# A decode step's tail: the MLP weights in two transfers, and its first layer moved among the steps that join the softmax parts

## The chip, the cores and the metric

The kernel runs on one NeuronCore of one Trainium2 chip. Its engines have their own instruction streams and meet at semaphores: TensorE (PE in the profile) multiplies matrices into the accumulator memory PSUM, VectorE (DVE) reduces and works elementwise, ScalarE (ACT) applies functions, GpSimd (POOL) does little here, SyncE (SP) issues the transfers. Sixteen DMA engines move data from the chip's memory into the on-chip memory SBUF. The metric is the device time of one execution in microseconds, lower is better.

## The reference

One decode step of two branches that share the input `x` (2 x 1 x 448), mixed by a gate that depends on `x`:

```python
q = (x @ wq) per head                       # wq: 448 x (16 x 256)
scores = q . k_cache * 256 ** -0.5          # k_cache: 2 x 16 x 4096 x 256
p = softmax(scores)
a = concat_heads(p @ v_cache) @ wo          # v_cache like k_cache; wo: 4096 x 448
b = relu(x @ w1) @ w2                       # w1: 448 x 1792, w2: 1792 x 448
g = sigmoid(sum(x * gate_w))
out = g * a + (1 - g) * b
```

All is float32. The two caches are by far the most data: 32 pairs of batch row and head, each with 4 MB of keys and 4 MB of values.

## The kernel before

**Units.** A pair of batch row and head is a unit; there are U = 32, run one after another. A unit's keys and values come in one transfer of 8192 KB into one of three slots (`slot[0..2]`, each 128 partitions x 65,536 bytes). PE computes the scores (L121): the 4096 positions lie as four groups of 1024, each with 32 equal rows, so `sc` is 128 x 1024. DVE takes the maximum (L135, into `nm`), ACT the exponential and its row sum (L128, into `p` and `ls`), and DVE multiplies `p` into eight pieces of the values with a running sum (L141, into `ov`). So each unit leaves partial maxima, sums and outputs for four groups of positions in `nm`, `ls` and `ov`, which are joined once at the end. The semaphore `freed` counts the units that are done; SP waits for it before it issues the transfer that reuses a slot (L166 in the loop, L169 to L172 for the last two units; the last unit comes as keys and values apart).

**The weights that follow.** When unit U-2 (counted from one) has freed slot 0, SP issues the MLP's matrices into it, both in one transfer `wm` (L174, semaphore `mlp_in`). When unit U-1 has freed slot 1, it issues the output matrix `wo` in six transfers (L178): 32 chunks of 448 columns, as 14 and 9 (`ACC`) and 4, 2, 2, 1 (`DIRECT`), each with a semaphore of its own (`wo_in`). All of these stand in one queue behind the cache's transfers. The last instruction of SP waits for the result and writes it out (L181).

**The tail, in PE's written order.** The order of each engine's work is the order in which the program lists it.

1. L225 to L234: wait for `wm`, then the first layer, 16 matmuls (32 instructions, as each float32 matmul is recorded as two) into `pa`; `c` runs over four pieces of the 448 inputs, `g` over four groups of hidden columns.
2. ACT: `hs` = relu, scaled by 1 - g (L315). PE: transposes of `hs` into `pb` (L237, L239). ACT: copies to `hr` (L317, L320).
3. L242 to L244: wait for the last unit (`freed` = U), then transposes of `nm` and `ls` into `pc`.
4. The joining: DVE takes the overall maximum per unit (`nb`, L352), ACT the factors `e` (L325, written behind the copies to `hr`), DVE the sum, its reciprocal and the weights `wb` (L354 to L358), PE spreads `wb` over the partitions by a matmul into `pa` (L255), DVE multiplies it into `ov` (`os`, L360), PE sums the four groups (L261), DVE expands the result to the operand `oc` (L363).
5. The second layer (L250), 14 matmuls into `acc`, is written in three portions: before L255, before L261 and after it.
6. The output matrix's first 23 chunks add to the same `acc` (L275), which holds four partial results in four groups of rows. DVE copies it to `a_sb` (L367). The matmul with `fold` (L283) adds the groups up into `z`.
7. The last 9 chunks go to `z` directly (L288), 8 instructions for each. `FOLD_AT = 1` puts L283 behind the first four of these chunks and ahead of the other five. DVE copies `z` to `res` (L369).

Of the kernel before, what the change touches and what calls it, by code (L numbers as in the profile page):

```python
# [4 lines left out]
AF = mybir.ActivationFunctionType  # L5
# [5 lines left out]
G = 4  # L11
# [2 lines left out]
CW = 512  # L14
ACC = (14, 9)
DIRECT = (4, 2, 2, 1)
FOLD_AT = 1


def gated_mix_decode(nc, wq, kv, wm, wo, out):  # L20
# [23 lines left out]
    def ev():  # L44
        sems.append(nc.alloc_semaphore(f"e{len(sems)}"))
        return sems[-1]
# [13 lines left out]

    out_sem = nc.alloc_semaphore("out_sem")
    slot_in = [ev() for _ in range(SLOTS)]
    last_v, mlp_in = ev(), ev()
    wo_in = [ev() for _ in ACC + DIRECT]
    scored, maxed, raised, queried, freed = (ev() for _ in range(5))

# [88 lines left out]
    with nc.Block(no_gpsimd_drain=True) as block:  # L155

        @block.sync
        def _(_e):
            sp.wait_ge(q_mm, 2)
            sp.dma_start(slot[0], kv[2]).then_inc(slot_in[0], 16)  # L160
            with nc.Fori(0, LOOP - 1, engines=(ET.SP,)) as r:
                u0 = sp.snap(r * SLOTS)
                for k in range(SLOTS):
                    s = (k + 1) % SLOTS
                    sp.wait_ge(freed, u0 + k + 1)
                    sp.dma_start(slot[s], kv[bass.ds(u0 + k + SLOTS, 1)].rearrange("o p n -> (o p) n")  # L166
                                 ).then_inc(slot_in[s], 16)
            sp.wait_ge(freed, U - 4)
            sp.dma_start(slot[1], kv[U - 2]).then_inc(slot_in[1], 16)  # L169
            sp.wait_ge(freed, U - 3)  # L170
            sp.dma_start(slot[2][:, :SW // 2], kv[U - 1][:, :SW // 2]).then_inc(slot_in[2], 16)
            sp.dma_start(slot[2][:, SW // 2:], kv[U - 1][:, SW // 2:]).then_inc(last_v, 16)  # L172
            sp.wait_ge(freed, U - 2)
            sp.dma_start(slot[0][:, :wm.shape[1]], wm).then_inc(mlp_in, 16)  # L174
            sp.wait_ge(freed, U - 1)
            k = 0
            for n, s in zip(ACC + DIRECT, wo_in):
                sp.dma_start(w_o[:, k * D:(k + n) * D], wo[:, k * D:(k + n) * D]).then_inc(s, 16)  # L178
                k += n
            sp.wait_ge(res_ok, 1)  # L180
            sp.dma_start(out, res[0:7 * 15 + 1:7, :]).then_inc(out_sem, 16)  # L181
# [8 lines left out]
        @block.tensor  # L190
        def _(_e):
            pe.wait_ge(x_ok, 1)
            for c in range(KC):
                r = rows_of(c)
                m = pe.matmul(pa[:, :1], x_of(r, c, P), xg[r, c, B:], start=(c == 0), stop=(c == KC - 1))  # L195
            m.then_inc(gate_mm, 1)
            W = 2 * KF * DH
            for i in range(2):
                w = slot[0][:, i * NW // 2:(i + 1) * NW // 2]
                if i:  # L200
                    pe.wait_ge(q_ok, i)
# [12 lines left out]
                for k in range(2 * T):  # L214
                    m = pe.transpose(pc[:, k * P:(k + 1) * P], q[:, k * P:(k + 1) * P], ident)
                m.then_inc(q_tr, 1)
            with nc.Fori(0, LOOP, 1, engines=(ET.PE,)) as r:
                for k in range(SLOTS):
                    s = (k + 1) % SLOTS
                    unit_pe(k, r * SLOTS + (k + 1), r * 16 + (32 if s == 0 else 16), s)  # L220
            for k in range(U - U1):
                s = (k + 1) % SLOTS
                unit_pe(k, U1 + k + 1, LOOP * 16 + 16, s)

            pe.wait_ge(mlp_in, 16)  # L225
            half = W1 // 2
            for c in range(KC):
                for g in range(G):
                    j, i = divmod(g, 2)
                    at = i * half + (j * KF + c if c < KF else 2 * KF) * FG  # L230
                    r = rows_of(c, j)
                    m = pe.matmul(pa[g * R:(g + 1) * R, :FG], x_of(r, c), w1[r, at:at + FG], start=(c == 0),  # L232
                                  stop=(c == KC - 1))
            m.then_inc(hid_mm, 1)  # L234
            pe.wait_ge(hid_ok, 1)
            for t in range(KF):
                pe.transpose(pb[:, t * P:(t + 1) * P], hs[:, t * P:(t + 1) * P], ident)  # L237
            for j in range(2):
                m = pe.matmul(pb[j * HP:(j + 1) * HP, KF * P:], hs[:, KF * P:], ident, start=True, stop=True)  # L239
            m.then_inc(hid_tr, 1)  # L240

            pe.wait_ge(freed, U)  # L242
            pe.transpose(pc[:U, :P], nm, ident)
            pe.transpose(pc[:U, P:2 * P], ls, ident).then_inc(ml_tr, 1)  # L244
            pe.wait_ge(hr_ok, 1)

            def mlp(lo, hi):
                for k in range(lo, hi):
                    g = k % G
                    pe.matmul(acc[g * R:(g + 1) * R, :D], hr[:, k, :], w2[:, k * D:(k + 1) * D], start=(k < G),  # L250
                              stop=False)

            mlp(0, 4)
            pe.wait_ge(wb_ok, 1)
            pe.matmul(pa[:, :U], wb.rearrange("u g r -> u (g r)"), ident[:U, :U], start=True,  # L255
                      stop=True).then_inc(wp_mm, 1)
            mlp(4, 8)
            pe.wait_ge(os_ok, 1)
            n = HH * B * J
            for g in range(G):  # L260
                m = pe.matmul(pc[g * R:(g + 1) * R, :n], sel,  # L261
                              os.rearrange("p u j -> p (u j)")[:, g * n:(g + 1) * n], start=True, stop=True)
            m.then_inc(po_mm, 1)
            mlp(8, NF)

            def o_of(k):
                return oc[:, k // J, k % J].rearrange("p r b -> p (r b)")

            pe.wait_ge(oc_ok, 1)
            k, n = 0, sum(ACC)  # L270
            for i, a in enumerate(ACC):
                pe.wait_ge(wo_in[i], 16)
                for _ in range(a):
                    g = k % G
                    m = pe.matmul(acc[g * R:(g + 1) * R, :D], o_of(k), w_o[:, k * D:(k + 1) * D], start=False,  # L275
                                  stop=(k >= n - G))
                    k += 1
            m.then_inc(acc_mm, 1)
            for i, a in enumerate(DIRECT):
                if i == FOLD_AT:  # L280
                    pe.wait_ge(a_ok, 1)
                    for g in range(G):
                        pe.matmul(z[g * R:(g + 1) * R, :DG], fold.rearrange("p r b -> p (r b)"), a_sb[:, g * DG:(g + 1) * DG], start=False,  # L283
                                  stop=False)
                pe.wait_ge(wo_in[len(ACC) + i], 16)
                for _ in range(a):
                    for g in range(G):
                        m = pe.matmul(z[g * R:(g + 1) * R, :DG], o_of(k),  # L288
                                      w_o[:, k * D + g * DG:k * D + (g + 1) * DG], start=(k == n),
                                      stop=(k == NO - 1))  # L290
                    k += 1
            m.then_inc(z_mm, 1)

        @block.scalar
        def _(_e):
# [15 lines left out]
                    unit_act(u, u + 1, (k + 1) % SLOTS, (k + 2) % SLOTS)  # L311
            for u in range(U1, U):
                unit_act(u, u + 1, (u + 1) % SLOTS, (u + 2) % SLOTS, u == U - 1)
            act.wait_ge(hid_mm, 1)
            act.activation(hs, pa[:, :FG], AF.Relu, scale=omg).then_inc(hid_ok, 1)  # L315
            act.wait_ge(hid_tr, 1)
# [8 lines left out]
            act.activation(e, pc[:U, 0:P:R], AF.Exp, bias=nb, scale=-1.0).then_inc(e_ok, 1)  # L325

        @block.vector
        def _(_e):
# [28 lines left out]
            dve.wait_ge(rl_ok, 1)  # L357
            dve.tensor_scalar(wb, e[:, :, None].to_broadcast([U, G, R]), rl, gp[:U], op0=ALU.mult, op1=ALU.mult).then_inc(wb_ok, 1)  # L358
            dve.wait_ge(wp_mm, 1)
            dve.tensor_tensor(os, ov, pa[:, :U, None].to_broadcast([P, U, J]), op=ALU.mult).then_inc(os_ok, 1)  # L360
            dve.wait_ge(po_mm, 1)
            for h in range(HH):
                m = dve.tensor_copy(oc[:, h], pc[:, h * B * J:(h + 1) * B * J].rearrange("p (o b j) -> p j o b", o=1, b=B)  # L363
# [66 lines left out]
```

## Time and profile before

| what | value |
|---|---|
| median of 3 runs | 677.75 us (677.21 to 677.79) |
| the profiled execution | 677.45 us |
| its span, first to last instruction | 675.9 us |
| moved by the main queue | 289.55 MB, 99.1% of 16 engines' span |
| busy: PE, DVE, ACT | 211.9, 340.4, 46.4 us |
| mean granted TensorE clock | 0.669 |

A busy engine is not the same as a late one: what counts is the chain of waits that ended last. In the rows of a timeline the first number is the start in us from the span's start, the second the duration, then engine, line, operation, tile written and tiles read, shapes and count. In the chain of waits the rows are start, duration, what. A DMA issue row gives the count, KB of each, and the us from issue to landing. A window's row gives its length, the busy time and instruction count of PE, of PE's weight loads (PEld), DVE, ACT and POOL, then the granted TensorE clock as a share of full speed, the DMA engines' share and GB/s.

### The profile page before, as it was taken

The page shows a single profiled execution, that of the slowest core. Times are in us where ns is not written, and L with a number is a line of the kernel's source. Part 1 is how long each engine was busy: PE and PEld are TensorE (multiplying, and loading weights), DVE is VectorE, ACT ScalarE, POOL GpSimd, SP SyncE. Part 2 cuts the span into 40 slices and gives each one's busy share as a digit, 9 for nine tenths or more (in the row PEclk, how much of TensorE's full clock was granted, in tenths as well). Part 3 has the DMA queues.
Part 4 walks back from the last instruction along what each step waited for, and adds up shares of the span by engine and source line. Part 5 has one row for each costly group of instructions (what it writes and reads, how often), then busy time and mean ns, then how long its engine had stood idle before and what let it go on. Part 6 is the DMA issues. An engine that isn't in the chain of part 4 may idle for free.

```text
span 675.9 us, 3969 instructions
## 1 busy us (share of the span) xinstructions
PE 211.9 (31%) x1309; PEld 52.0 (8%) x1309; DVE 340.4 (50%) x563; ACT 46.4 (7%) x107; POOL 0.7 (0%) x6
## 2 busy tenths in 40 slices
PE   0742211323332122333322133333212333332427
PEld 0210000000000000000000000000000000000003
DVE  0015566554455666445556654545566554465742
ACT  0010000000000000000000000000000000000101
POOL 0000000000000000000000000000000000000000
PEclk9976567677665667766566776765567676665659
DMA  9999999999999999999999999999999999999996
GB/s 380 434 431 435 431 434 434 434 434 434 434 434 434 434 434 434 434 434 434 434 434 434 434 434 434 434 434 434 434 434 434 434 434 434 434 434 431 449 407 275
DMA packets 5940, 289.61 MB, mean 429 GB/s; under 512 B 688, under 2 KB 816, under 8 KB 1200
## 3 DMA queue, kind: packets, MB, share of 16 engines
q1 hardware_dynamic: 5936, 289.55, 99.1%
q8 instruction: 3, 0.05, 0.0%
q14 instruction: 1, 0.01, 0.0%
HBM read 289.54 MB, written 0.01 MB: 428 GB/s over the span
## 4 chain that ended last, share of the span: by engine, by line
DMA 69%; PE 12%; DVE 12%; issue 6%; DVEq 1%; ACT 1%; ACTq 0%; SPq 0%
DMA slot<-in_kv 61%; DVE slot L141 9%; PE sc L121 8%; DMA slot<-in_wm 5%; DMA slot<-in_wq 3%; DVE nm L135 2%; PE pb L206 1%; PE pa L232 1%; PE acc L275 1%; DVEq L141 1%; ACT p L128 0%; PE pa L195 0%; PE z L288 0%; DVE oc L363 0%; ACTq L307 0%
## 5 line engine op out<-in xcount | busy, mean ns | idle before, releaser
L141 DVE SCALAR_TENSOR_TENSOR slot<-slot,p 128x1024 f32<-128x1024 f32 x256 | 295.9, 1221 | 47.1 <-ACT p L128 47.1
L121 PE MATMUL sc<-slot,qc 128*32 128x512 f32 x1024 | 181.5, 874 | 419.4 <-DMA slot<-in_kv 419.4
L135 DVE TENSOR_REDUCE nm<-sc 128x1024 f32 (+1 forms) x32 | 39.2, 1225 | 243.9 <-PE sc L121 243.9
L121 PEld LDWEIGHTS sc<-slot,qc 128*32 128x32 f32 x1024 | 41.0, 153 | 559.2 <-issue 539.7
L128 ACT ACTIVATE p<-sc,nm 128x1024 f32<-128x1024 f32 x32 | 35.7, 1114 | 563.2 <-DVE nm L135 563.2
L141 DVE DVE_READ_ACCUMULATOR slot<-slot,p (+1 forms) x256 | 21.2, 83 | 0.0
L232 PE MATMUL pa<-slot,xr 128*32 128x448 f32 (+1 forms) x32 | 5.4, 826 | 18.7 <-DMA slot<-in_wm 18.7
L206 PE MATMUL pb<-slot,xr 128*32 128x512 f32 (+1 forms) x64 | 10.0, 763 | 0.0
L335 DVE COPY xr<-slot 128x512 f32<-128x512 f32 x1 | 0.4, 427 | 18.1 <-DMA slot<-in_wq 18.1
L195 PE MATMUL pa<-slot,xr 128*128 128x1 f32 (+1 forms) x8 | 1.9, 356 | 20.8 <-DVE xr L335 20.8
L352 DVE TENSOR_REDUCE nb<-pc 32x1 f32<-32x4 f32 x1 | 0.1, 149 | 12.6 <-PE pc L244 12.6
L128 ACT ACTIVATION_READ_ACCUMULATOR p<-sc,nm (+1 forms) x32 | 6.2, 193 | 0.0
L130 ACT ACTIVATE qc<-qt 128x2 f32 (+1 forms) x31 | 6.0, 192 | 0.0
L275 PE MATMUL acc<-slot,oc 128*32 128x448 f32 x46 | 4.7, 541 | 0.0
L250 PE MATMUL acc<-slot,hr 128*32 128x448 f32 x28 | 3.5, 546 | 0.6 <-ACT hr L320 0.6
L195 PEld LDWEIGHTS pa<-slot,xr 128*128 128x128 f32 (+1 forms) x8 | 1.8, 320 | 20.8 <-DVE xr L335 20.8
L367 DVE COPY a_sb<-acc 128x448 f32<-128x448 f32 x1 | 0.6, 625 | 4.8 <-PE acc L275 4.8
L232 PEld LDWEIGHTS pa<-slot,xr 128*32 128x32 f32 (+1 forms) x32 | 1.1, 150 | 23.1 <-DMA slot<-in_wm 19.6
L206 PEld LDWEIGHTS pb<-slot,xr 128*32 128x32 f32 (+1 forms) x64 | 2.0, 129 | 6.4 <-issue 6.3
L288 PE MATMUL z<-slot,oc 128*32 128x112 f32 x72 | 2.5, 260 | 0.0
L315 ACT ACTIVATE hs<-pa,omg 128x448 f32<-128x448 f32 x1 | 0.6, 634 | 19.9 <-PE pa L232 19.9
L288 PEld LDWEIGHTS z<-slot,oc 128*32 128x32 f32 x72 | 2.0, 110 | 0.5 <-issue 0.5
(45 smaller groups left out, 17.8 us busy)
## 6 DMA issues: line engine op xcount, KB each, us to landing
slot<-in_kv SPq DMA_DIRECT2D x2, 4096.0 KB, 34.5
slot<-in_wq SPq DMA_DIRECT2D x1, 7174.0 KB, 19.6
slot<-in_wm SPq DMA_DIRECT2D x1, 6272.0 KB, 36.3
slot<-in_wo SPq DMA_DIRECT2D x1, 3136.0 KB, 24.2
slot<-in_wo SPq DMA_DIRECT2D x1, 2016.0 KB, 28.6
slot<-in_wo SPq DMA_DIRECT2D x1, 896.0 KB, 30.2
slot<-in_wo SPq DMA_DIRECT2D x2, 448.0 KB, 31.2
slot<-in_kv SPq DMA_DIRECT2D x31, 39.9
```

The source lines that it names most:

```text
L121: m = pe.matmul(sc[g * R:(g + 1) * R, c * CW:(c + 1) * CW], qc[:, s, t:t + 1].to_broadcast([P, R]), slot[s][:, lo:lo + CW], start=(t == 0) ...
L128: act.activation(p, sc, AF.Exp, bias=nm[:, bass.ds(u, 1)], accum_out=ls[:, bass.ds(u, 1)]).then_inc(raised, 1)
L130: act.activation(qc[:, s_next, :], qt[:, bass.ds(u + 1, 1), :].rearrange("p o t -> p (o t)"), AF.Copy).then_inc(queried, 1)
L135: dve.tensor_reduce(nm[:, bass.ds(u, 1)], sc, axis=AX.X, op=ALU.max, negate=True).then_inc(maxed, 1)
L141: m = dve.scalar_tensor_tensor(v, v, 1.0, p, op0=ALU.mult, op1=ALU.mult, accum_out=ov[:, bass.ds(u, 1), j].rearrange("p o -> p o"))
L195: m = pe.matmul(pa[:, :1], x_of(r, c, P), xg[r, c, B:], start=(c == 0), stop=(c == KC - 1))
L206: m = pe.matmul(pb[g * R:(g + 1) * R, :], x_of(r, c), w[r, at:at + CW], start=(c == 0), stop=(c == KC - 1))
L232: m = pe.matmul(pa[g * R:(g + 1) * R, :FG], x_of(r, c), w1[r, at:at + FG], start=(c == 0), stop=(c == KC - 1))
L250: pe.matmul(acc[g * R:(g + 1) * R, :D], hr[:, k, :], w2[:, k * D:(k + 1) * D], start=(k < G), stop=False)
L275: m = pe.matmul(acc[g * R:(g + 1) * R, :D], o_of(k), w_o[:, k * D:(k + 1) * D], start=False, stop=(k >= n - G))
L288: m = pe.matmul(z[g * R:(g + 1) * R, :DG], o_of(k), w_o[:, k * D + g * DG:k * D + (g + 1) * DG], start=(k == n), stop=(k == NO - 1))
L315: act.activation(hs, pa[:, :FG], AF.Relu, scale=omg).then_inc(hid_ok, 1)
```

## The change

The MLP's matrices come in two transfers with a semaphore each, `w1` first. The first layer is written ahead of the joining: its first two pieces of inputs stand before the wait for the last unit, the third between the transposes of `nm` and `ls` and the wait for `wb`, the fourth between the `wb` matmul and the wait for `os`. The sum over groups (L261 before) follows, then relu, transposes and copies, and the second layer in one piece behind the waits for `w2` and `hr`. The `wb` matmul goes to `pb` instead of `pa`, since `pa` is in use by the first layer; DVE reads it there. ACT's `e` stands ahead of the relu. `FOLD_AT` is 0: the folded sums come ahead of all direct chunks, and start the sum in `z`. The number of matmuls is the same.

```diff
-FOLD_AT = 1
+FOLD_AT = 0
...
-            sp.dma_start(slot[0][:, :wm.shape[1]], wm).then_inc(mlp_in, 16)
+            sp.dma_start(w1, wm[:, :W1]).then_inc(w1_in, 16)
+            sp.dma_start(w2, wm[:, W1:]).then_inc(w2_in, 16)
...
-            pe.wait_ge(mlp_in, 16)
             half = W1 // 2
...
-            m.then_inc(hid_mm, 1)
+
+            def hidden(lo, hi):
+                for c in range(lo, hi):
+                    for g in range(G):
+                        j, i = divmod(g, 2)
+                        at = i * half + (j * KF + c if c < KF else 2 * KF) * FG
+                        r = rows_of(c, j)
+                        m = pe.matmul(pa[g * R:(g + 1) * R, :FG], x_of(r, c), w1[r, at:at + FG], start=(c == 0),
+                                      stop=(c == KC - 1))
+                return m
+
+            pe.wait_ge(w1_in, 16)
+            hidden(0, 2)
+            pe.wait_ge(freed, U)
+            pe.transpose(pc[:U, :P], nm, ident)
+            pe.transpose(pc[:U, P:2 * P], ls, ident).then_inc(ml_tr, 1)
+            hidden(2, 3)
+            pe.wait_ge(wb_ok, 1)
+            pe.matmul(pb[:, :U], wb.rearrange("u g r -> u (g r)"), ident[:U, :U], start=True,
+                      stop=True).then_inc(wp_mm, 1)
+            hidden(3, 4).then_inc(hid_mm, 1)
+            pe.wait_ge(os_ok, 1)
+            n = HH * B * J
+            for g in range(G):
+                m = pe.matmul(pc[g * R:(g + 1) * R, :n], sel,
+                              os.rearrange("p u j -> p (u j)")[:, g * n:(g + 1) * n], start=True, stop=True)
+            m.then_inc(po_mm, 1)
             pe.wait_ge(hid_ok, 1)
             for t in range(KF):
                 pe.transpose(pb[:, t * P:(t + 1) * P], hs[:, t * P:(t + 1) * P], ident)
...
-            pe.wait_ge(freed, U)
-            pe.transpose(pc[:U, :P], nm, ident)
-            pe.transpose(pc[:U, P:2 * P], ls, ident).then_inc(ml_tr, 1)
+            pe.wait_ge(w2_in, 16)
             pe.wait_ge(hr_ok, 1)
...
-            mlp(0, 4)
-            pe.wait_ge(wb_ok, 1)
...
-            mlp(4, 8)
-            pe.wait_ge(os_ok, 1)
...
-            mlp(8, NF)
+            for k in range(NF):
+                g = k % G
+                pe.matmul(acc[g * R:(g + 1) * R, :D], hr[:, k, :], w2[:, k * D:(k + 1) * D], start=(k < G),
+                          stop=False)
...
-                                      w_o[:, k * D + g * DG:k * D + (g + 1) * DG], start=(k == n),
+                                      w_o[:, k * D + g * DG:k * D + (g + 1) * DG], start=(k == n and FOLD_AT > 0),
...
+            act.wait_ge(nb_ok, 1)
+            act.activation(e, pc[:U, 0:P:R], AF.Exp, bias=nb, scale=-1.0).then_inc(e_ok, 1)
             act.wait_ge(hid_mm, 1)
             act.activation(hs, pa[:, :FG], AF.Relu, scale=omg).then_inc(hid_ok, 1)
...
-            act.wait_ge(nb_ok, 1)
-            act.activation(e, pc[:U, 0:P:R], AF.Exp, bias=nb, scale=-1.0).then_inc(e_ok, 1)
...
-            dve.tensor_tensor(os, ov, pa[:, :U, None].to_broadcast([P, U, J]), op=ALU.mult).then_inc(os_ok, 1)
+            dve.tensor_tensor(os, ov, pb[:, :U, None].to_broadcast([P, U, J]), op=ALU.mult).then_inc(os_ok, 1)
```

More of the change, by code (lines that the diff above doesn't have):

```diff
@@ L62, in gated_mix_decode @@
     slot_in = [ev() for _ in range(SLOTS)]
-    last_v, mlp_in = ev(), ev()
+    last_v, w1_in, w2_in = ev(), ev(), ev()
     wo_in = [ev() for _ in ACC + DIRECT]
@@ L223, in _ @@
                 unit_pe(k, U1 + k + 1, LOOP * 16 + 16, s)
-            pe.wait_ge(mlp_in, 16)
             half = W1 // 2
[L227 to L233, printed above, removed]
-            m.then_inc(hid_mm, 1)
+            def hidden(lo, hi):
[23 more added lines that the diff above has]
+            m.then_inc(po_mm, 1)
             pe.wait_ge(hid_ok, 1)
@@ L240, in _ @@
             m.then_inc(hid_tr, 1)
-            pe.wait_ge(freed, U)
-            pe.transpose(pc[:U, :P], nm, ident)
-            pe.transpose(pc[:U, P:2 * P], ls, ident).then_inc(ml_tr, 1)
+            pe.wait_ge(w2_in, 16)
             pe.wait_ge(hr_ok, 1)
[L247 to L251, printed above, removed]
-            mlp(0, 4)
-            pe.wait_ge(wb_ok, 1)
-            pe.matmul(pa[:, :U], wb.rearrange("u g r -> u (g r)"), ident[:U, :U], start=True,
-                      stop=True).then_inc(wp_mm, 1)
-            mlp(4, 8)
-            pe.wait_ge(os_ok, 1)
[L259 to L263, printed above, removed]
-            mlp(8, NF)
+            for k in range(NF):
+                g = k % G
+                pe.matmul(acc[g * R:(g + 1) * R, :D], hr[:, k, :], w2[:, k * D:(k + 1) * D], start=(k < G),
+                          stop=False)
             def o_of(k):
@@ L282, in _ @@
                     for g in range(G):
-                        pe.matmul(z[g * R:(g + 1) * R, :DG], fold.rearrange("p r b -> p (r b)"), a_sb[:, g * DG:(g + 1) * DG], start=False,
-                                  stop=False)
+                        pe.matmul(z[g * R:(g + 1) * R, :DG], fold.rearrange("p r b -> p (r b)"),
+                                  a_sb[:, g * DG:(g + 1) * DG], start=(i == 0), stop=False)
                 pe.wait_ge(wo_in[len(ACC) + i], 16)
```

## The prediction

> **What bounds the kernel now.** I read the page first, then the chain of waits in order of time from the last cache units on, then the timeline of the same stretch, the DMA issues with their landings, and last the windows for the granted clock.
>
> ```profile
> span 675.9 us, 3969 instructions
> ...
> q1 hardware_dynamic: 5936, 289.55, 99.1%
> ```
>
> One queue keeps its engines busy for 99.1% of the span. 289.55 MB are unchanged by the edit, so only what stands behind the last bytes, or between them and the end, can be won. The chain of the last 60 us:
>
> ```profile
> 618.61 36.30 DMA slot<-in_wm
> ...
> 654.96 5.42 PE pa L232 x32
> ...
> 660.40 0.64 ACT hs L315
> ...
> 661.09 0.55 PE pb L237 x3
> ...
> 662.05 0.49 ACT hr L317
> ...
> 662.90 0.26 ACT e L325
> ...
> 663.56 0.34 DVE wb L358
> 663.95 0.40 PE pa L255 x2
> ...
> 665.42 1.43 DVE oc L363 x4
> ...
> 666.89 4.08 PE acc L275 x41
> ```
>
> The whole MLP transfer lands at 618.61 + 36.30 = 654.91. From there it is one serial chain on PE, ACT and DVE (first layer, relu, transposes, softmax joining, expansion into `oc`), until L275 may start at 666.89. The tail of it, from the timeline:
>
> ```profile
> 671.66 0.62 DVE L367 COPY a_sb<-acc 128x448 f32<-128x448 f32 x1 [4.82 <-PE acc L275]
> 672.34 0.40 PE L283 MATMUL z<-a_sb,fold 128*32 128x112 f32 x8
> 672.56 1.14 PE L288 MATMUL z<-slot,oc 128*32 128x112 f32 x40
> 673.77 0.28 DVE L369 COPY res<-z 128x112 f32<-128x112 f32 x1 [1.48 <-PE z L288]
> 674.07 0.60 SPq L181 DMA_DIRECT2D out<-res  x1
> ```
>
> The last z matmul ends at 672.56 + 1.14 = 673.70; 2.2 us later the span is over, and 1.55 us lie outside it (the profiled execution took 677.45). Against it stand the landings of the output matrix. The issues one after another, from the timeline of SP, and then the DMA issues with their sizes and the us to landing (a median where there are two):
>
> ```profile
> 638.15 0.33 SPq L178 DMA_DIRECT2D slot<-in_wo  x1
> 638.52 0.43 SPq L178 DMA_DIRECT2D slot<-in_wo  x1
> 639.00 0.43 SPq L178 DMA_DIRECT2D slot<-in_wo  x1
> 639.47 0.43 SPq L178 DMA_DIRECT2D slot<-in_wo  x1
> 639.94 0.91 SPq L178 DMA_DIRECT2D slot<-in_wo  x2
> ```
>
> ```profile
> slot<-in_wo SPq DMA_DIRECT2D x1, 3136.0 KB, 24.2
> slot<-in_wo SPq DMA_DIRECT2D x1, 2016.0 KB, 28.6
> slot<-in_wo SPq DMA_DIRECT2D x1, 896.0 KB, 30.2
> slot<-in_wo SPq DMA_DIRECT2D x2, 448.0 KB, 31.2
> ...
> slot<-in_wo SPq DMA_DIRECT2D x1, 224.0 KB, 31.5
> ```
>
> Issue plus landing gives: A0 (14 chunks) 662.35, A1 (9) 667.12, D0 (4) 669.20, D1 and D2 (2 each) about 670.67 and 671.14, D3 (1) 640.42 + 31.5 = 671.92, where 640.42 is 639.94 + 0.91 - 0.43. So A0 lies there for 4.5 us before L275 begins, and at D3's landing PE still has the fold and 40 z matmuls ahead. The end is now set by the chain, by 673.70 - 671.92 = 1.78 us over the last landing. That is the most that the edit can touch.
>
> **The change part by part.** *The split transfer.* One more issue on SP, 0.33 us by the row of the first L178 issue. It stands behind the wait for unit U-2 (618.61) and ahead of the wait that ends at 638.15, so 19 us of waiting hide it; with that cover gone it would delay the output matrix by 0.33 us. In the queue, w1 is 3136 KB, as large as A0, which took 662.35 - 654.91 = 7.44 us; so w1 lands near 647.47 and w2 still near 654.91. The price in the stream of one more transfer is shown by no row alone. From below, nothing: the six L178 transfers carry 7168 KB (7.34 MB) in 671.92 - 654.91 = 17.01 us, 431 GB/s, against 428 GB/s if 289.55 MB are put over the whole span. From above, D3's 0.229 MB took about 0.78 us where 431 GB/s would make 0.53: 0.25 us. I take 0.05, nearer to the large transfers, since w1 and w2 are as large as A0.
>
> *The first layer ahead of the joining.* The instructions stay the same 32; they start at 647.5 instead of 654.96, on a clock of half speed:
>
> ```profile
> 655.71 0.20 PEld L232 LDWEIGHTS pa<-slot,xr 128*32 128x32 f32 x4 [0.55 <-issue]
> ...
> 657.95 0.20 PEld L232 LDWEIGHTS pa<-slot,xr 128*32 128x32 f32 x4 [0.55 <-issue]
> ```
>
> Twelve in 657.95 - 655.71 = 2.24 us are 0.187 each at half clock. Sixteen take 3.0 us: 650.5. The next wait is for the last unit, and the joining starts with two transposes:
>
> ```profile
> 648.56 1.22 DVE L141 SCALAR_TENSOR_TENSOR slot<-slot,p 128x1024 f32<-128x1024 f32 x1
> ...
> 662.37 0.15 DVE L352 TENSOR_REDUCE nb<-pc 32x1 f32<-32x4 f32 x1 [12.58 <-PE pc L244]
> ```
>
> That unit is done at 648.56 + 1.22 = 649.78, so the transposes are held 0.7 us by the first layer, at no cost as long as `oc` is ready by 662.35. Then, with the durations above: transposes 0.4 (before, `nb` followed at 662.37 on PE's earlier work done by 662.05): 650.9; `nb` 0.15, `e` 0.26, and from `e`'s end to `wb`'s 663.90 - 663.16 = 0.74, with small gaps 1.25: 652.2. Meanwhile eight of the first layer take 1.5: 652.4. From the `wb` matmul's start to `oc`'s it was 665.42 - 663.95 = 1.47, for that matmul, `os` and L261; I give 1.0 to the first two, beside which the last eight run (to about 654.2), and 0.47 to L261 behind them; `oc` 1.43: 656.1. That is 10.8 us sooner than 666.85 and 6 us ahead of A0. The MLP: `hs` 0.64, transposes 0.96 to 1.5, `hr` 0.85 make about 657; w2 has landed 2 us before; 28 matmuls of L250 take 2.8 us at full clock, 5.4 at half: 659.8 to 662.4. ACT's moved `e` waits for `nb` with the relu behind it; `nb` is there 3 us before the first layer ends, so nobody waits longer. DVE's read of `pb` in place of `pa` has the same shape.
>
> *What is late next.* The transfers. A0 at 662.35: 28 instructions. L275 shows 41 in 4.08 us, 0.1 each, so 2.8 us: 665.2, 1.9 us before A1. A1 at 667.12: 18 instructions, 2.0 with the last one's latency: 669.2. The order of the fold is the one part that speaks against the edit: before, the 32 z matmuls of D0 ran while DVE copied `acc`; now nothing runs from 669.2 on but that copy (671.66 to 672.34 in the rows above, 0.68 to the fold's first matmul, with 0.05 ahead of it): fold at 669.95. Fold and last 40 took 673.70 - 672.34 = 1.36 us for 48, with about 0.16 of latency 0.025 each. Eight plus 72 make 2.0: PE would be through at 671.95 + 0.16 = 672.1 if nothing were awaited. D3 lands at 671.92; 0.05 to start (654.91 to 654.96 above), 8 x 0.025 and 0.16 make 672.33. So D3 sets the end, with PE 0.2 us ahead. **Sum:** 672.33 - 673.70 = -1.37, plus 0.05 for the split: -1.32, and 677.45 - 1.32 = 676.1 us. The profiled execution lies 0.3 below the median of 677.75 and inside the runs' 677.21 to 677.79; the chain's end must scatter with the clock (below), so I leave the sum at its own execution.
>
> **The clock, and the rivals.** The windows, cut where the granted clock changes:
>
> ```profile
> 604.48:607.90 3.42, 1.97 (x20) 0.37 (x12) 1.22 (x1) 0.00 (x0) 0.00 (x0) 1.00 0.80 345
> 607.90:611.31 3.41, 0.00 (x0) 0.00 (x0) 1.98 (x3) 1.30 (x3) 0.00 (x0) 1.00 0.75 327
> ...
> 624.97:628.39 3.42, 1.32 (x12) 0.12 (x4) 1.23 (x1) 0.76 (x1) 0.00 (x0) 1.00 0.91 393
> 628.39:631.80 3.41, 1.72 (x11) 0.41 (x15) 2.93 (x5) 0.54 (x3) 0.00 (x0) 0.50 0.96 413
> 631.80:635.21 3.41, 3.41 (x22) 0.79 (x18) 3.41 (x7) 0.00 (x0) 0.00 (x0) 0.50 1.06 456
> 635.21:638.63 3.42, 1.03 (x12) 0.12 (x4) 3.42 (x7) 0.00 (x0) 0.00 (x0) 1.00 1.20 517
> ...
> 655.69:659.11 3.42, 3.42 (x24) 0.79 (x16) 0.00 (x0) 0.00 (x0) 0.00 (x0) 0.50 0.94 403
> 659.11:662.52 3.41, 2.46 (x21) 0.77 (x17) 0.15 (x1) 1.10 (x3) 0.00 (x0) 1.00 0.98 421
> ```
>
> The clock changes only at steps of 3.413 us. A window with PE busy for 1.97 us (58%) kept the full clock in the next, one with 1.32 (39%) lost it; one with 1.72 (50%) did not regain it, a full one did. Where the steps fall against the kernel differs between executions, by up to 3.4 us.
>
> *Rival A: the clock falls while PE waits for the output matrix.* It has two places. Between L250's end (659.8) and A0 (662.35) lie 2.5 us without work: a window around them loses the clock, and if the next one begins near 661 it holds 662.4 to 664.4 only, 2.0 us or 58%, which need not regain it (50% didn't): A0 then takes 28 x 0.187 = 5.2 us, to 667.6, and A1 starts late and slow. And a window that ends at any point from 667.2 to 668.6 holds the same sum of A0's rest (665.2 less its start) and A1's beginning: 665.2 - 667.17 + 3.41 = 1.44 us, 42%, between the 39% that lost the clock and the 58% that kept it. A1 at half clock costs up to 18 x 0.087 = 1.6 us, of which 0.2 is slack: 677.5; with half of A1 slow 676.7. For it: the 39% row. Against it: other positions hold well over half. The first place takes some 0.6 of 3.41 us of positions, the second 1.4 at a coin's toss: 1.3 of 3.41, a little over a third, and not all of these with a price that shows. Price 676.6 to 677.6.
>
> [...]
>
> *Rival B, the other side: the low clock lasts to the end.* If the clock falls before A1 and the copy of `acc` (0.73 us without PE work) keeps the following window under the level that raises it (between 50% and 100%), then A1 takes 18 x 0.187 + 0.2 = 3.6 us (670.8), the fold begins at 671.5, and 80 z matmuls at 0.05 make 4.0: 675.7, 2.0 after now's 673.70: 679.5. It decides from the point at which that window holds under some 2.2 us; A1 itself fills more of it, which speaks against.
>
> *Rival C: the split costs the stream.* If one more transfer takes as much as the whole of D3 did, 0.78 us, every landing behind w1 comes later by that: 677.45 - 1.37 + 0.78 = 676.9, no change that can be told. For it: small D3 took half again its share by bytes. Against it: the six transfers together kept 431 GB/s.
>
> [...]
>
> *Rival D: the gain is there, but the last landing moves.* If the wait for D3 weren't the end but w2's or A0's part were late (PE at half clock throughout L250 and A0: 662.4 + 5.4 = 667.8), A1 would start 0.6 late and the end come at about 677, the same verdict as A.
>
> **How the numbers follow.** Forecast 676.1: 0.56. A: 0.26, at 676.6 to 677.6. D: 0.04. C: 0.07. B: 0.07. The forecast's own range is 675.7 (landings 0.4 sooner, as the runs scatter by 0.58) to 676.5. A measurement of this kernel can tell some 0.2% from no change: 1.36 us, so faster begins at 676.4; the forecast lies just 0.3 beyond, and I give 0.49 of its 0.56 and 0.03 of A to faster. Same: the rest of A and the forecast, D and C, 0.41. Slower: B, 0.07. The range goes from 675.5 to 677.6, which leaves out B and some of each edge.
>
> **What would show each step.** Right: two landings, w1 near 647.5 and w2 near 654.9; L363 ending near 656; L275 starting within 0.1 of A0's landing near 662.4; the copy of `acc` near 669.3; the last eight z matmuls within 0.5 us after D3's landing near 671.9; span near 674.6. Wrong: D3 landing at 672.2 or later (C); a granted clock of 0.50 in a window after 664 with L275 at 0.187 each (A), still so at the z matmuls (B); L275 starting long after A0's landing (D). A span of 675.5 or more makes the prediction wrong.

## The result, and the profile after

The changed kernel takes 676.03 us (median of 16 runs, 675.77 to 676.69) against 677.53 us for the kernel before (16 runs, 676.39 to 678.08). The ratio is 0.9981 with a 95% interval of 0.9974 to 0.9989: 1.3 us less by the ratio, 1.5 by the medians. The forecast was 676.1. The gain is clear of noise. By the ratio it falls just short of the 0.2% at which the prediction let "faster" begin, by the medians it lies just beyond. Agreement to 0.1 us is partly luck, since the runs of this one kernel are spread over 0.9 us.

The profiled execution took 675.96 us. From its page, the span and the main queue:

```profile
span 674.4 us, 3971 instructions
...
q1 hardware_dynamic: 6080, 289.55, 99.3%
```

The tail of the changed kernel from the timelines (start, duration, engine, line; the bracket is the idle time before, and what ended it):

```profile
637.47 2.70 SPq L179 DMA_DIRECT2D slot<-in_wo  x6
...
647.34 3.21 PE L234 MATMUL pa<-slot,xr 128*32 128x448 f32 x16 [12.26 <-DMA slot<-in_wm]
...
653.97 1.42 DVE L364 COPY oc<-pc 128x256 f32<-128x256 f32 x4 [0.74 <-PE pc L251]
...
656.34 3.20 PE L264 MATMUL acc<-slot,hr 128*32 128x448 f32 x28 [1.01 <-ACT hr L323]
...
662.23 3.20 PE L276 MATMUL acc<-slot,oc 128*32 128x448 f32 x28 [2.69 <-DMA slot<-in_wo]
...
666.90 2.44 PE L276 MATMUL acc<-slot,oc 128*32 128x448 f32 x18 [1.47 <-DMA slot<-in_wo]
...
669.38 0.62 DVE L368 COPY a_sb<-acc 128x448 f32<-128x448 f32 x1 [13.99 <-PE acc L276]
...
670.06 0.40 PE L284 MATMUL z<-a_sb,fold 128*32 128x112 f32 x8 [0.72 <-DVE a_sb L368]
...
670.27 1.91 PE L289 MATMUL z<-slot,oc 128*32 128x112 f32 x72
...
672.25 0.28 DVE L370 COPY res<-z 128x112 f32<-128x112 f32 x1 [2.25 <-PE z L289]
```

The first layer starts at 647.34, 7.6 us sooner than before. The expanded operand `oc` is ready at 655.39, and PE is idle for 2.7 us until the output matrix's first piece releases it at 662.23. Where the kernel before had one serial chain from 654.91 to the end, here PE waits for arrivals three times: for w1, A0 and A1. The DMA issues, with KB each and the us from issue to landing:

```profile
slot<-in_wm SPq DMA_DIRECT2D x2, 3136.0 KB, 31.2
slot<-in_wo SPq DMA_DIRECT2D x1, 3136.0 KB, 24.6
slot<-in_wo SPq DMA_DIRECT2D x1, 2016.0 KB, 29.0
...
slot<-in_wo SPq DMA_DIRECT2D x1, 224.0 KB, 32.0
```

The last issue began at 637.47 + 2.70 - 0.43 = 639.74 (its issue took 0.43), so D3 lands at 671.74. The z matmuls end at 670.27 + 1.91 = 672.18, 0.44 later, near the 0.41 (0.05 + 8 x 0.025 + 0.16) that the prediction estimated for a start, eight matmuls and their latency. PE's own chain from A1 (copy, fold, 72 matmuls without a pause) ends at the same moment: a tie. The profile's chain of waits (start, duration, what) leads back to A1 and not to D3:

```profile
637.84 29.02 DMA slot<-in_wo
...
666.90 2.46 PE acc L276 x18
```

So in this execution two arrivals set the end together: A1 at 666.86 with 5.3 us of work behind it, and D3 at 671.74 with 0.44.

### The profile page after: what moved, and what is told of

The parts are those of the page before. It is cut to its first block, busy times and chain, and to the rows that moved or that the text cites. A ratio compares the mean times of both kernels' runs of the same rounds, so it can differ in the third digit from the quotient of the medians.

```text
span 674.4 us, 3971 instructions
## 1 busy us (share of the span) xinstructions
PE 218.0 (32%) x1309; PEld 53.4 (8%) x1309; DVE 340.4 (50%) x563; ACT 46.3 (7%) x107; POOL 0.7 (0%) x6
## 3 DMA queue, kind: packets, MB, share of 16 engines
q1 hardware_dynamic: 6080, 289.55, 99.3%
## 4 chain that ended last, share of the span: by engine, by line
DMA 70%; DVE 13%; PE 10%; issue 6%; ACT 1%; DVEq 1%; SPq 0%; ACTq 0%
DMA slot<-in_kv 65%; DVE slot L141 11%; PE sc L121 9%; DMA slot<-in_wo 4%; DVE nm L135 2%; ACT p L128 1%; DVEq L141 1%; PE acc L276 0%; PE z L289 0%; SPq L166 0%; DVE a_sb L368 0%; DVEq L135 0%; ACTq L128 0%; PE z L284 0%; SPq L67 0%
## 5 line engine op out<-in xcount | busy, mean ns | idle before, releaser
L121 PE MATMUL sc<-slot,qc 128*32 128x512 f32 x1024 | 187.2, 898 | 413.1 <-DMA slot<-in_kv 413.1
L276 PE MATMUL acc<-slot,oc 128*32 128x448 f32 x46 | 5.6, 542 | 4.2 <-DMA slot<-in_wo 4.2
L276 PEld LDWEIGHTS acc<-slot,oc 128*32 128x32 f32 x46 | 1.7, 109 | 8.1 <-issue 5.8
L364 DVE COPY oc<-pc 128x256 f32<-128x256 f32 x4 | 1.4, 418 | 0.7 <-PE pc L251 0.7
## 6 DMA issues: line engine op xcount, KB each, us to landing
slot<-in_wo SPq DMA_DIRECT2D x1, 3136.0 KB, 24.6
```

Source lines behind the costliest of these rows:

```text
L121: m = pe.matmul(sc[g * R:(g + 1) * R, c * CW:(c + 1) * CW], qc[:, s, t:t + 1].to_broadcast([P, R]), slot[s][:, lo:lo + CW], start=(t == 0) ...
```

## The experiments

Each kernel was timed beside the kernel before, whose medians in the three sets of runs were 677.36, 677.61 and 677.44 us.

**The split alone**, the order untouched:

```diff
-            sp.dma_start(slot[0][:, :wm.shape[1]], wm).then_inc(mlp_in, 16)
+            sp.dma_start(w1, wm[:, :W1]).then_inc(w1_in, 16)
+            sp.dma_start(w2, wm[:, W1:]).then_inc(w2_in, 16)
...
-            pe.wait_ge(mlp_in, 16)
+            pe.wait_ge(w1_in, 16)
...
+            pe.wait_ge(w2_in, 16)
             mlp(0, 4)
```

> The kernel before with the MLP's matrices in two transfers, PE waiting for w1 ahead of the first layer and for w2 ahead of the second; nothing else is moved. Theory 1 (a floor of arrivals: whatever lets the expanded operand and the second layer be done before the first piece of the output matrix lands near 662.2 ends with that matrix's last landing): the first layer starts at 647.4, relu and transposes are done near 655, the joining runs behind them to about 659.5, the second layer to about 660, so it ends as the changed kernel does: 676.0, within 0.3, and 1.5 under the kernel before. Theory 2 (the order among the joining's steps carries the gain, the split only lets it): the joining still stands behind the first layer, so at most half of the gain, 676.8 or more.

Measured: 676.08 us (675.84 to 676.49), ratio 0.9981 (0.9972 to 0.9990), the whole gain of the change. From its timelines:

```profile
647.82 5.12 PE L233 MATMUL pa<-slot,xr 128*32 128x448 f32 x32 [12.11 <-DMA slot<-in_wm]
...
658.04 1.42 DVE L365 COPY oc<-pc 128x256 f32<-128x256 f32 x4 [0.61 <-PE pc L263]
...
662.72 7.28 PE L277 MATMUL acc<-slot,oc 128*32 128x448 f32 x43 [3.26 <-DMA slot<-in_wo]
```

The joining still stands behind the first layer, `oc` comes 4 us later than in the changed kernel (659.46), and PE still waits 3.26 us for the output matrix. The order among the joining's steps is not needed for the gain; theory 2 falls. The loading of the last eight z matmuls' weights (PEld) shows what the end waits for, D3, which was issued 2.27 us after A0 (2.70 - 0.43) and landed at 637.90 + 2.27 + 32.1 = 672.27:

```profile
672.34 0.16 PEld L290 LDWEIGHTS z<-slot,oc 128*32 128x32 f32 x8 [0.19 <-DMA slot<-in_wo]
```

The clock fell ahead of A0 in this execution, for two windows:

```profile
661.68:665.10 3.42, 2.38 (x16) 0.86 (x20) 0.00 (x0) 0.00 (x0) 0.00 (x0) 0.50 1.04 448
665.10:668.52 3.42, 3.42 (x24) 1.31 (x20) 0.00 (x0) 0.00 (x0) 0.00 (x0) 0.50 0.93 381
```

That is what the prediction's rival A describes. At 0.187 each, A0's 28 instructions last from 662.72 to about 667.9, past A1's landing at 637.90 + 0.37 + 29.1 = 667.37 (the second issue starts 0.37 us behind the first), and the copy of `acc` starts 3.05 us after that landing (670.42), against 2.5 in the changed kernel's profile. With the fold behind the first direct chunks this cost nothing. With the fold ahead of all of them it would have ended 2.80 us after the copy's start, as in the changed kernel (672.18 - 669.38): at 673.22, where the last z matmul here ended at 671.31 + 1.43 = 672.74. That is an estimate of 0.5 us.

**The order alone**, with one transfer (the changed kernel with `w1_in` and `w2_in` put back to one `mlp_in`):

```diff
-            sp.dma_start(w1, wm[:, :W1]).then_inc(w1_in, 16)
-            sp.dma_start(w2, wm[:, W1:]).then_inc(w2_in, 16)
+            sp.dma_start(slot[0][:, :wm.shape[1]], wm).then_inc(mlp_in, 16)
```

> The changed kernel with one transfer for both matrices, so PE's new order has to wait for it near 654.9. Theory 1: the first layer and with it the joining start at 654.96; the operand is ready near 663, but relu, transposes and copies end near 663.9, the second layer near 666.9, the two pieces of the output matrix near 671.5, the copy 672.2, and fold with 72 matmuls 674.4: 0.7 later than the kernel before, 678.2 (677.8 to 678.6). Theory 2 (the order carries the gain): at or below 676.8.

Measured: 678.12 us (677.86 to 678.92), ratio 1.0011 (1.0003 to 1.0020). From its chain of waits (start, duration, what):

```profile
655.26 3.22 PE pa L233 x16
...
667.79 4.55 PE acc L274 x40
...
672.37 0.64 DVE a_sb L366
...
673.45 1.77 PE z L287 x72
```

The order written for an early w1 makes the joining wait for a late one, and the copy of `acc` stands uncovered on the chain: slower than the kernel before, and within the range that theory 1 gave.

**The joining first, one transfer**: all steps of the joining ahead of the wait for `mlp_in`, fold where it was.

```diff
+            pe.wait_ge(freed, U)
+            pe.transpose(pc[:U, :P], nm, ident)
+            pe.transpose(pc[:U, P:2 * P], ls, ident).then_inc(ml_tr, 1)
+            pe.wait_ge(wb_ok, 1)
...
+            m.then_inc(po_mm, 1)
             pe.wait_ge(mlp_in, 16)
```

> The kernel before with the whole joining written ahead of the first layer (the factor e ahead of the relu on ACT, the spread weights in pb), one transfer for both matrices and the fold behind the first direct piece as before. Theory 1: the joining runs under the wait for the transfer and is done near 654; first layer 655.0 to 660.4, copies to 662.9, second layer to 665.6, the output matrix's two pieces without a pause to 670.2, and the fold with the last 40 matmuls to 672.4: 1.3 under the kernel before, 676.2, with a wider scatter than the changed kernel (0.5 and more), since the first layer starts at half clock on the path. Theory 3 (the early arrival of w1 is what gains): no change, 677.3 or more.

Measured: median 676.23 us, but in two groups: 7 of 12 runs at 675.84 to 676.28, four at 678.4 to 678.9 and one at 680.9; so the ratio is 1.0002 (0.9987 to 1.0017). The first group is where theory 1 put it: an early w1 isn't needed either, theory 3 falls. The second group no theory had. Of its members, the run at 680.9 has the lowest mean granted clock of the twelve (0.594); no profile shows it. Two more kernels went after it: the same once more, and one with spare matmuls into `acc` (which the second layer starts anew) in PE's waits ahead of the first layer.

```diff
+            pe.wait_ge(raised, U)
+            spare(36)
             pe.wait_ge(freed, U)
...
+            spare(6)
             pe.wait_ge(wb_ok, 1)
...
+            spare(2)
             pe.wait_ge(os_ok, 1)
...
+            spare(9)
             pe.wait_ge(mlp_in, 16)
```

> The kernel with the joining first and one transfer once more, unchanged, for the clock of another execution. Theory 5: the runs fall into the same two groups; if the profiled one is of the upper group, its windows show a granted clock of 0.50 in second layer and output matrix (0.187 per instruction) and PE, not the last landing, ending last.

> The kernel with the joining first and one transfer, of which 7 of 12 runs had ended at 675.8 to 676.3 and 4 at 678.4 to 678.9 (and one at 680.9), with spare matmuls into acc (which the second layer starts anew) in PE's waits ahead of the first layer: 36 behind the last exponential, 6, 2 and 9 in the joining's and the transfer's waits. Theory 5 (the two groups are the clock: where its steps fall unluckily the chain from the first layer on runs at half clock past the landing of the output matrix): the first layer runs at full clock, 3.4 us instead of 4.9, and the upper group is gone: all runs at 675.8 to 676.6. Rival (something else than the clock makes the upper group): some three runs in ten at 678 or more again.

Measured: unchanged, 7 of 10 runs at 675.98 to 676.54 and three at 678.36 to 679.24 (ratio 0.9989, 0.9977 to 1.0000); with the spare matmuls all 11 at 675.82 to 676.63 (median 676.23, ratio 0.9982, 0.9972 to 0.9991). The profiled execution of the unchanged one was of the upper group (679.24). Its windows, cut at the clock's steps (length, busy time of PE, PEld, DVE, ACT, POOL, granted clock, DMA share, GB/s):

```profile
657.60:661.02 3.42, 3.42 (x24) 0.47 (x16) 0.00 (x0) 0.00 (x0) 0.00 (x0) 0.50 0.97 416
661.02:664.43 3.41, 1.72 (x19) 0.72 (x19) 0.00 (x0) 1.44 (x4) 0.00 (x0) 1.00 1.04 447
664.43:667.85 3.42, 3.42 (x24) 0.92 (x18) 0.00 (x0) 0.00 (x0) 0.00 (x0) 0.50 0.91 383
667.85:671.26 3.41, 3.41 (x40) 1.24 (x38) 0.00 (x0) 0.00 (x0) 0.00 (x0) 1.00 0.82 328
```

The first layer (655.23 to 661.37) ran at half clock up to its last 0.4 us; the clock then rose, for the very window in which PE waits for relu and copies, was lost again, and the second layer ran at half clock. The output matrix behind it ran at full clock (the last row), where the expectation had half. Theory 5 holds for these two groups: where the clock falls in the first two layers moves the end by 2 us and more, and with the spare matmuls (granted clock 1.00 from 646 to 648.8 us and from 660 on in that profile, the first layer 4.05 us instead of 6.14) the upper group is gone. It differs from the prediction's rivals A and B in the place, ahead of the output matrix, where here nothing waits for arrivals.

**The fold's place**, in the changed kernel put back to `FOLD_AT = 1`, and in the kernel before put to 0:

> The changed kernel with the fold behind the first four direct chunks, as it was before the change. Theory 1: in the changed kernel's profile PE's own chain (copy, fold, 72 matmuls) ends at 672.18, and the last landing near 671.74 allows 672.15, a tie; with the fold later the 32 matmuls run under the copy, PE has about 0.7 us more room, so the median stays within 0.1 of the changed kernel's 676.03, and the slow end of its runs (676.4 to 676.7) comes down by 0.3 or more. Theory 4 (the folded sums ahead of the direct chunks were a part of the gain): slower than the changed kernel by 0.3 or more.

Measured: 676.24 us (675.87 to 676.88), ratio 0.9983 (0.9974 to 0.9992). The median lies 0.2 above 676.03 and 0.06 above the changed kernel's second measurement below, which neither theory forecast; by the ratios the two can't be told apart. The slow end did not come down, against theory 1: 0.7 us more room on PE gains nothing. The last matmuls of its profile wait for landings, the last eight among them for D3 (their weights load from 672.18, D3 landed at 672.11):

```profile
671.64 0.94 PE L289 MATMUL z<-slot,oc 128*32 128x112 f32 x24 [0.47 <-DMA slot<-in_wo]
```

> The kernel before with nothing but the folded sums ahead of all direct chunks. Theory 1: in the kernel before PE's chain sets the end, and the 32 matmuls of the first direct piece ran while DVE copied acc; now they stand behind the copy, so the end comes 0.6 to 0.8 later: 678.0 (677.8 to 678.4). Theory 4 (the fold's place was a part of the gain): 677.2 or less.

Measured: 678.33 us (677.34 to 679.01), 0.7 above its kernel before by the medians, ratio 1.0008 (0.9999 to 1.0017), which by itself does not exclude no change. From its timelines:

```profile
671.22 0.62 DVE L367 COPY a_sb<-acc 128x448 f32<-128x448 f32 x1 [4.82 <-PE acc L275]
...
672.12 1.91 PE L288 MATMUL z<-slot,oc 128*32 128x112 f32 x72
```

From the copy's start to the last matmul's end it is 674.03 - 671.22 = 2.81 us, against 673.70 - 671.66 = 2.04 in the kernel before: 0.77 on a chain that nothing covers. Where arrivals set the end, the same move costs nothing that shows in the runs.

**The clock in the waits for the output matrix**: the changed kernel with 11 spare matmuls behind the second layer and 5 between the output matrix's first two pieces.

> The changed kernel with spare matmuls of 448 columns into the idle score memory: 11 behind the second layer (2.5 us of the 2.7 us in which PE waits for the output matrix's first piece) and 5 between its first two pieces (1.4 of 1.5 us). They add nothing to the result. Theory 5 (the clock's fall in these waits makes the slow end of the changed kernel's runs): the runs gather at 675.8 to 676.1, none above 676.4, median 675.95. Rival (the scatter is that of the landings): the same spread as the changed kernel, 675.8 to 676.7, and a median within 0.15 of 676.05.

Measured: 676.40 us (675.76 to 677.43), ratio 0.9984 (0.9975 to 0.9993). No narrower, rather wider; theory 5 fails for this kernel, and the rival's spread and median (within 0.15 of 676.05) are missed as well. In its profile the clock stayed full through the tail (granted 1.00 from 660 to 674.8 us). The last of the spare matmuls, from the timeline, and the landing of the second piece:

```profile
665.42 1.98 PE L270 MATMUL sc<-slot,hr 128*32 128x448 f32 x8
```

```profile
slot<-in_wo SPq DMA_DIRECT2D x1, 2016.0 KB, 29.2
```

They ended at 667.40, 0.06 behind that landing (issued at 638.14, so 667.34); that spares at a lower clock ran past a landing in the slowest runs is argued only.

**More transfers**: w2 in 14 of 224 KB.

```diff
-            sp.dma_start(w2, wm[:, W1:]).then_inc(w2_in, 16)
+            for i in range(NF):
+                sp.dma_start(w2[:, i * D:(i + 1) * D], wm[:, W1 + i * D:W1 + (i + 1) * D]).then_inc(w2_in, 16)
```

> The changed kernel with w2 in 14 transfers of 224 KB, 13 more in the queue (SP's issues, 14 times some 0.45 us, fit into its wait of 18 us). At nothing for each: 676.0. At the 0.05 that the prediction took: 676.7. At the bound of 0.25 from the last small piece: 679.3. [...] I expect 676.7, with the last landing about 0.65 later than in the changed kernel.

Measured: 676.52 us (676.42 to 677.06), ratio 0.9984 (0.9975 to 0.9993). By the medians that is 0.3 to 0.5 above the changed kernel (676.03 and 676.18), by the ratios (0.9981 and 0.9985) it can't be told from it. The landings are the cleaner measure: the last piece of w2 landed at 646.64 + 8.7 = 655.34, 7.9 us behind w1 (618.65 + 28.8 = 647.45), against 7.4 to 7.5 in the six profiles with w2 in one transfer. That is some 0.5 us for 13 transfers, 0.04 each. Against the expectation, SP's issues did not fit into its wait:

```profile
619.02 28.06 SPq L176 DMA_DIRECT2D slot<-in_wm  x14
...
621.87 12.61 SPq L176 DMA_DIRECT2D slot<-in_wm  x1
...
647.12 0.97 SPq L180 DMA_DIRECT2D slot<-in_wo  x1
```

**Without the second piece's matmuls** (the 18 instructions of L276 behind A1 left out, so their part of the sum is missing):

> The changed kernel without the 9 chunks of the output matrix's second piece on PE (18 instructions left out, their part of the sum is missing; the transfer stays), so that copy and fold are done 2.5 us sooner and only landings are left. Theory 1 (the last landing is the floor): no faster than 675.9, median 675.85 to 676.05. Rival (PE's chain from the second piece through copy, fold and 72 matmuls is what is left, as the changed kernel's chain of waits has it): 0.3 or more under the changed kernel, 675.7 or less.

Measured: 676.23 us (675.78 to 676.77), ratio 0.9978 (0.9969 to 0.9987). With 2.5 us less work on PE's chain the median is no lower than the changed kernel's 676.18 of the third set; it is 0.2 above the range of theory 1, and the rival's 675.7 did not come. The profile is less clean than the expectation had it, since PE, idle for 2.5 us ahead of the direct chunks, lost its clock at the end (granted 1.00 up to 670.6 us, 0.50 behind it):

```profile
671.29 1.35 PE L292 MATMUL z<-slot,oc 128*32 128x112 f32 x24 [0.40 <-DMA slot<-in_wo]
```

These 24 take 1.35 us instead of the 0.94 above, and the time (676.39) is 4.6 us above its last landing at 671.78, 0.4 more than elsewhere. If most of its runs lost the clock like this, up to 0.4 us from PE's chain could hide behind it. The cleaner evidence against that chain is the later fold above.

**The changed kernel again:**

> The changed kernel itself beside the two others. Theory 1: 676.0 to 676.3, and the profiled time lies 4.2 above the last landing of the output matrix, as it did in five profiles of kernels that wait for it (671.74 to 672.46, 675.96 to 676.65).

Measured: 676.18 us (675.89 to 676.78), ratio 0.9985 (0.9976 to 0.9994). Its profile (676.47) shows what rival A described. First the windows, then the timeline:

```profile
658.93:662.34 3.41, 1.12 (x10) 0.14 (x2) 0.00 (x0) 0.00 (x0) 0.00 (x0) 1.00 0.91 389
662.34:665.76 3.42, 3.02 (x20) 0.98 (x24) 0.00 (x0) 0.00 (x0) 0.00 (x0) 0.50 0.99 423
665.76:669.17 3.41, 3.40 (x33) 1.01 (x26) 0.00 (x0) 0.00 (x0) 0.00 (x0) 1.00 0.99 404
```

```profile
638.29 2.70 SPq L179 DMA_DIRECT2D slot<-in_wo  x6
...
662.75 7.12 PE L276 MATMUL acc<-slot,oc 128*32 128x448 f32 x46 [2.69 <-DMA slot<-in_wo]
...
670.80 1.91 PE L289 MATMUL z<-slot,oc 128*32 128x112 f32 x72
```

```profile
slot<-in_wo SPq DMA_DIRECT2D x1, 2016.0 KB, 28.7
...
slot<-in_wo SPq DMA_DIRECT2D x1, 224.0 KB, 31.7
```

The window of the wait for A0 holds 33% of work, the clock is lost, and A0 starts at a granted clock of 0.50; but the window that it fills raises the clock again, and A0 is through at 667.42, 0.06 behind A1's landing (638.29 + 0.37 + 28.7 = 667.36). The price is nothing that shows: D3 lands at 640.56 + 31.7 = 672.26, and the time is 4.21 above.

**Landings and times together.** The last landing worked out in the same way (last issue's start plus the us to landing) in the profiles, that without the second piece's matmuls aside:

| kernel | last landing | profiled time | difference |
|---|---|---|---|
| joining first, warm | 671.62 | 675.95 | 4.33 |
| changed | 671.74 | 675.96 | 4.22 |
| joining first | 671.81 | 676.02 | 4.21 |
| changed, fold later | 672.11 | 676.32 | 4.21 |
| changed, again | 672.26 | 676.47 | 4.21 |
| split alone | 672.27 | 676.49 | 4.22 |
| spare matmuls | 672.44 | 676.62 | 4.18 |
| w2 in 14 | 672.46 | 676.65 | 4.19 |
| before | 671.92 | 677.45 | 5.53 |
| before, fold 0 | 672.20 | 677.81 | 5.61 |
| order alone | 672.39 | 678.92 | 6.53 |
| joining first, again | 672.23 | 679.24 | 7.01 |

In the first eight the time is the last landing plus 4.2 to 4.3 us, however the work is ordered. A1 lands a nearly fixed time ahead of D3 (4.9 us in both profiles of the changed kernel), so the table by itself doesn't tell the two apart. The loads of the last eight matmuls' weights do: in five of the eight (joining first, joining first warm, fold later, split alone, spare matmuls) they are released by D3, 0.02 to 0.07 us behind its landing. In the other three, the changed kernel twice and w2 in 14, nothing waits behind A1's matmuls, and PE's chain from there ends together with D3's. The landing itself scatters by 0.8 us between these profiles, by 0.5 between the two of the changed kernel, and the time with it. In the last four PE's chain sets the end.

## Why the prediction was right, point by point

**The floor** of arrivals held: "D3 sets the end" is what five profiles show, while in the changed kernel itself D3 and PE's chain from A1 tie. The forecast's 4.2 us from the last landing to the end (677.45 - 1.37 - 671.92 = 4.16) is the measured difference. Single terms: w1 landed at 619.62 + 27.7 = 647.32 and w2 at 620.00 + 34.7 = 654.70, against 647.5 and 654.9; first layer 647.34 against 647.5; `oc` 655.39 against 656.1; L276 from 662.23, 0.16 behind A0's landing (637.47 + 24.6 = 662.07) and not within 0.1; copy at 669.38 against 669.3; z's end 672.18 against 672.33, with PE's chain in a tie and not 0.2 ahead. The forecast missed the profiled execution by 0.14, and the landing alone, 671.74 where 671.92 was carried over, makes 0.18. That it did not lie further off is luck: in the second profile of the same kernel D3 landed at 672.26.

**The split's cost**, 0.05, was of the right size: some 0.04 for each of the smaller pieces of w2. Rival C falls, and so does the upper bound of 0.25. Both rested on a reading of the median of D1 and D2 as D2's own landing. By itself, D2 of the kernel before took 31.5 us and landed at 639.94 + 31.5 = 671.44, so D3 came 0.48 us behind it and not 0.78, which is no more than its 0.53 by bytes. In a queue that was busy for 99.3% of the span (the profile with w2 in 14) 13 more transfers of 224 KB moved the last landing of w2 by 0.5 us.

**The moved first layer and joining** were costed at nothing, rightly; but the runs show that the change holds two remedies of which either would do. The split alone reaches the floor, and so does the joining alone in most runs. The new order is only a gain with the split: by itself it lost 0.8 us by the medians.

**The fold** ahead of the direct chunks was named as the part that speaks against the edit: 0.77 in the profile of the kernel where the chain sets the end, nothing measurable in the changed one. By the estimate at the split alone it would cost some 0.5 in an execution that loses the clock for two windows ahead of A0.

**Rival A** was mis-sized: its mechanism came true, its price did not. "A0 then takes 28 x 0.187 = 5.2 us, to 667.6, and A1 starts late and slow": in the changed kernel's second profile A0 took 4.67, for the window that it fills (3.02 of 3.42 us, 88%) gave the clock back before it was through, and A1 started on time at full clock. In the split alone the whole passage came true, and the end still followed D3. The fall ahead of A0 is not rare either: of the six profiles that wait for A0 behind an early w1 without spare matmuls, four show it (split alone, fold later, w2 in 14, changed again), where the prediction gave this place 0.6 of 3.41 us of positions.

The first profile of the changed kernel was close to such a fall, with 1.48 us of work in its window from 658.06 to 661.47. Of 27 runs of the changed kernel four lie at 676.65 to 676.78, at the low edge of the 676.6 to 677.6 that had a chance of 0.26, and none above. The kernel with the later fold, which has room for such a fall, is spread as wide (675.87 to 676.88), so the scatter is that of the landings as far as the profiles show; the slowest runs were not profiled. The prediction's signs of A (half clock after 664) and of C (D3 at 672.2 or later) both stood in the second profile, whose time (676.47) lay within the forecast's own range all the same: these signs don't decide.

**Rival B** and **D**: no run of the changed kernel reached 677, let alone 679.5. The forecast lay 0.3 us beyond the edge at which "faster" begins, which is why the 0.52 for faster and the 0.41 for the same stood so near to each other; the ratio's -0.19% lies at that edge, on the side of the same.

The gain stands at some 1.3 us because before, the chain's end lay 1.3 (5.53 - 4.2) over the floor; nothing in the runs beats the floor, and what makes the last landing scatter stays open.

## What to carry to other kernels

Where one queue is busy to the end, put the last landing beside the last matmul first: their distance, less what must follow a landing, is all that reordering can win, and more than one order wins all of it. Being ready just before the last large piece lands is not enough: here the orders that began with the output matrix by 664.51 ended with the landings, and the kernel before, which began at 666.89 with both A0 and A1 still to do and A1 landing at 667.12, lost 1.3 us. A step that stands uncovered on such a chain (here the copy ahead of the fold) cost nothing that showed once arrivals set the end, and its full length before. Judge a wait on TensorE by how the work in each window of the clock adds up, since a burst that fills the next one can buy the clock back: here the clock came back after one that was filled to 88% (3.02 us, the changed kernel again) and not after one of 70% (2.38 us, the split alone).

## What was not expected of the hardware

The clock was lost after a window with more work than another that held it. In the kernel before, this window held with 1.42 us of work, 42%:

```profile
508.92:512.33 3.41, 1.42 (x16) 0.20 (x8) 1.23 (x1) 0.46 (x1) 0.00 (x0) 1.00 0.75 327
512.33:515.70 3.37, 0.00 (x0) 0.00 (x0) 2.48 (x5) 0.84 (x3) 0.00 (x0) 1.00 1.39 603
```

In the profile of the kernel before all 75 changes of the granted clock lie within 0.04 us of a grid of 3.413 us, in the changed kernel's all 76 do. Cut along this grid, the units of both first profiles, 30 to 640 us with nearly only score matmuls on PE (178 windows each), show a sharp edge: from full clock every window with 1.42 us or more held it, every one with 1.40 or less lost it; from half clock none with 2.58 or less regained it, every one with 2.70 or more did. The 2.2 us that the prediction's rival B took for the latter was an estimate, and too low. The window from 661.02 to 664.43 above does not fit: it lost the clock with 1.72 us, 50%. What differs is the kind of work: in it some 0.9 us are transposes and the small matmuls beside them. Whether that is the cause was not shown: no run here took them away alone.

SP's issues are not always 0.43 us. With w2 in 14 transfers one issue took 12.61 us and all fourteen 28.06, with no wait in the program between them, only earlier transfers in the queue; the output matrix was issued 9.6 us later than in the changed kernel (647.12 against 637.47) and A0 still landed 7.38 us behind the last of w2 (655.34 to 662.72), as in the changed kernel (654.70 to 662.07, 7.37).
